# Sink probabilities, sink values and the order of a step in a sliding-window attention stage that runs ahead of two feed-forward layers

## The chip, the cores and the metric

The kernel runs on one core of a Trainium2 chip. The metric is the device time of one execution in microseconds, as the median of several runs.

## The reference, cut to what matters

```python
def _attn_ref(q, k, v, n_sink, window):          # q, k, v: (2, 8, 768, 64)
    scores = scale * np.matmul(q, k.transpose(0, 1, 3, 2))
    keep = (pos[None, :] < n_sink) | ((rel >= 0) & (rel < window))   # n_sink 4, window 128
    scores = np.where(keep, scores, -1000000000.0)
    a = np.exp(scores - np.max(scores, axis=-1, keepdims=True))
    a = a / (np.sum(a, axis=-1, keepdims=True) + 1e-09)
    return np.matmul(a, v)
x = attention rearranged to (1536, 512)
x = ((x @ w_a) * (x @ w_b)) @ w_out               # d_ff 1536
return np.maximum(x @ w_in, 0.0) ** 2 @ w_out2     # d_ff 2048
```

The feed-forward weights arrive as float64.

## The kernel before, in words

Attention is cut into 24 groups: a batch, a block of 128 queries, and four heads. A query block sees its own and the previous key block and the first eight keys, the sink. The loop of `attention_fast` runs steps g = 0 to 25. Each step works on several groups at once: `scores(g)` and `softmax(g, 0)`, `softmax(g, 1)`, the transposes of the probabilities of group g-1 (`probs`, `probs_copy`), the transposes of k and q of group g+1 (`transposes`), `normalize(g)`, the value products of group g-2 (`values`) and the transpose of the sink probabilities of g-1 (`probs_sink`). On TensorE, VectorE, ScalarE and GpSimd the order of the instructions in this stage is that of the program; the SP queue, which issues the loads, may be ordered otherwise.

In a softmax, VectorE selects the live triangle of the two key blocks in PSUM (L265), takes each head's maximum (L268), and ScalarE takes the exponential (L271). `normalize` (L280 to L288) divides on VectorE; GpSimd then splits the sink columns into two rounded parts (L287, L288). `probs_copy` copies the transposed probabilities on ScalarE (`th`, L302), and GpSimd cuts them into two triangles with two selects (`lu`, L309 and L311). The sink values are laid out once in `vs` (L183 to L207): two loads, splits on GpSimd, four matmuls that place them, two products on VectorE.

Two other works are woven into a step. First, the decode of the float64 weights, one tile of 128x512 in each step that `DECODE` lists: `W.stages` has ScalarE take a magnitude (L503), VectorE do four operations (L505 to L510), ScalarE cast the high part (`wh`, L515) and VectorE subtract it (`wl`, L517). The words `next(piece)` in the loop say where each part is issued. Second, `fill`, twice in a step: 12 matmuls of the first feed-forward layer (`psa`, L562) with one decoded tile. From step 6 on, when 256 tokens of attention are ready, each `fill` takes the next tile: tiles 0 and 1 in step 6, 2 and 3 in step 7, 4 and 5 in step 8, 6 and 7 in step 9. Its third matmul is the first to need `wl`. In every second `fill` VectorE multiplies the two results (`gs`, L576). Before step 6, and where no tokens are ready, `fill` issues two warming matmuls.

After the attention stage TensorE runs the feed-forward layers, and `W.ahead` decodes the remaining tiles, a third as often as TensorE's pieces come.

Of the kernel before, what the change touches and what calls it, by code (L numbers as in the profile page):

```python
# [18 lines left out]
P = 128  # L19
SK = 8  # L20
# [6 lines left out]
DECODE = (1, 2, 3, 4, 5, 6, 7, 8, 10, 12, 14, 16, 18, 20)  # L27
SINK = (0, 1, 3)
# [26 lines left out]
def setup(tc, cp, tp, n_sink, window):  # L55
    nc = tc.nc
    c = Attn()
    ident = tp.tile([P, P], F32, name="ident")
    make_identity(nc, ident)
    c.identr = cp.tile([P, P], F32R, name="identr")  # L60
    nc.vector.tensor_copy(c.identr, ident)
    c.ident = c.identr.bitcast(F32)

    raw = cp.tile([P, 4], I32, name="raw")
    nc.scalar.dma_start(raw[:, 0:2], n_sink.bitcast(I32).partition_broadcast(P))
    nc.scalar.dma_start(raw[:, 2:4], window.bitcast(I32).partition_broadcast(P))
    warm = tp.tile([P, 1], F32, name="warm")
    nc.scalar.activation(warm, c.ident[:, 0:1], AF.Exp)
    lo = cp.tile([P, 2], F32, name="lo_f")
    hi = cp.tile([P, 2], F32, name="hi_f")  # L70
    nc.vector.tensor_copy(lo, raw.bitcast(U32)[:, 0:4:2])
    nc.vector.tensor_copy(hi, raw[:, 1:4:2])
    par = cp.tile([P, 2], F32, name="par")
    nc.vector.scalar_tensor_tensor(out=par, in0=hi, scalar=4294967296.0, in1=lo, op0=ALU.mult, op1=ALU.add)
    c.ns = par[:, 0:1]
    c.w = par[:, 1:2]

    return c
# [51 lines left out]
def attention_fast(tc, ctx, c, rp, spare, q, k, v, xh, xl, fill, decode, warm):  # L130
# [54 lines left out]
    def sink_parts():
        for t, part, off in ((sel[0], slice(0, 64), slice(64, 96)), (sel[1], slice(64, 96), slice(0, 64))):
            t_ = t[:, part].rearrange("p (a s) -> p a s", s=SK)
            nc.gpsimd.tensor_copy(t_, c.ident[0:SK, 0:SK].unsqueeze(1).to_broadcast(t_.shape))
            nc.gpsimd.tensor_copy(t[:, off], c.ident[0:SK, P - (off.stop - off.start):P])
        nc.vector.tensor_reduce(out=own, in_=c.ident[0:96, 0:96].rearrange("p (k j s) -> p j k s", k=3, s=SK),  # L190
                                op=ALU.add, axis=AX.XY)

        vsr = raws.pop("s")
        for b in range(B):
            hi, lo = (t[0:SK] for t in spare[b])
            src = vsr[:, b].rearrange("p h d -> p (h d)")
            nc.gpsimd.tensor_copy(hi, src)
            nc.gpsimd.tensor_sub(lo, src, hi.bitcast(F32))

    def sink_values():  # L200
        for b in range(B):
            hi, lo = (t[0:SK] for t in spare[b])
            pt = ps_t.tile([P, 512], F32, name="pvs", tag="tr")
            nc.tensor.matmul(pt[0:96], lhsT=sel[0], rhs=hi, start=True, stop=False)
            nc.tensor.matmul(pt[0:96], lhsT=sel[1], rhs=lo, start=False, stop=True)
            nc.vector.tensor_mul(vs[:, b].rearrange("p (g q) (r d) -> p g (q r) d", g=2, r=2),
                                 pt[0:96].rearrange("p (g j d) -> p g j d", g=2, d=D),  # L207
                                 own.unsqueeze(1).unsqueeze(3).to_broadcast([96, 2, 4, D]))
# [231 lines left out]
class Weights:  # L440
# [7 lines left out]
    def __init__(self, tc, cp, rp, w_a, w_b, w_out, w_in2, w_out2):  # L448
# [30 lines left out]
        self.beat = 0  # L479

# [10 lines left out]
    def stages(self):  # L491

        while len(self.raws) < AHEAD and self.next < len(self.order):
# [9 lines left out]
        nc.scalar.activation(tf, up.bitcast(F32), AF.Abs)  # L503
# [3 lines left out]
                                op0=ALU.logical_shift_left, op1=ALU.bitwise_or)  # L507
        nc.vector.scalar_tensor_tensor(out=t, in0=up, scalar=0x3FFFFFFF, in1=t,  # L508
# [161 lines left out]
def sliding_window_moe_kernel(ctx, tc, q, k, v, n_sink, window, w_a, w_b, w_out, w_in2, w_out2, out):  # L670
# [16 lines left out]
    with tc.tile_pool(name="mk", bufs=1, side="right") as mk:  # L687
        c = setup(tc, cp, mk, n_sink, window)
        masks(tc, cp, mk, c)

    def run(attend):
# [3 lines left out]
        with ExitStack() as c0:  # L695
# [51 lines left out]
    run(lambda ctx, *work: attention_fast(tc, ctx, c, rp, first[-3:], q, k, v, xh, xl, *work))  # L747
# [39 lines left out]
```

## Time and profile before

| | |
|---|---|
| median of 3 runs (lowest, highest) | 687.59 us (687.39, 688.04) |
| the profiled execution, its own time | 688.03 us |
| its span, first to last instruction | 686.0 us |
| busy: TensorE, VectorE, ScalarE, GpSimd | 658.2, 406.0, 274.9, 48.8 us |

The profiled execution took 0.44 us more than the median, and 2.03 us of it lie outside the span. The busy times are sums over stages with different limits: the attention stage ends at 177 us, and from 200 us on TensorE is busy without a gap until the last stores.

### The profile page before, as it was taken

What the parts mean: (1) busy time and instruction counts of PE and PEld (TensorE: products, weight loads), DVE (VectorE), ACT (ScalarE), POOL (GpSimd) and SP (SyncE); (2) the same over time, 40 slices, a digit from 0 to 9 for tenths busy, and PEclk for the clock granted to TensorE, in tenths of its full rate; (3) what the DMA queues carried; (4) which work ended last, traced back from release to release, by engine and by line L of the source; (5) the groups of instructions that cost most, each with busy time, mean ns of one, the idle gap of its engine ahead of it and who ended that gap; (6) DMA issues with size and microseconds to landing.
All of it is one profiled execution on the core that took longest, in us unless ns stands there. A gap on an engine that the chain in (4) does not pass through costs nothing.

```text
span 686.0 us, 9622 instructions
## 1 busy us (share of the span) xinstructions
PE 658.2 (96%) x3582; PEld 546.0 (80%) x3582; DVE 406.0 (59%) x921; ACT 274.9 (40%) x638; POOL 48.8 (7%) x100
## 2 busy tenths in 40 slices
PE   6869999989999999999999999999999999999996
PEld 3557887878988888888888888888888888888884
DVE  5999778786688811389932599624933232323323
ACT  4565566564544511455521356234532222222221
POOL 3132222223000000000000000000000000000000
PEclk9799999999999999999999999999999999999999
DMA  9654343341065400044600024300200000001011
GB/s 193 167 134 125 101 116 87 108 116 32 16 194 159 152 5 0 1 135 145 189 23 1 28 86 136 119 1 27 67 1 0 1 0 1 1 0 62 11 51 66
DMA packets 65413, 48.96 MB, mean 71 GB/s; under 512 B 39760, under 2 KB 60240, under 8 KB 65360
## 3 DMA queue, kind: packets, MB, share of 16 engines
q1 hardware_dynamic: 65072, 48.28, 24.6%
q8 instruction: 30, 0.49, 0.3%
q14 instruction: 23, 0.19, 0.1%
q10 hardware_dynamic: 288, 0.00, 0.0%
HBM read 45.12 MB, written 3.15 MB: 70 GB/s over the span
## 4 chain that ended last, share of the span: by engine, by line
PE 88%; DVE 7%; DMA 2%; issue 1%; ACT 1%; SPq 0%; POOL 0%; DVEq 0%; POOLq 0%
PE psa L562 46%; PE acc L600 33%; PE x L330 2%; PE sc L250 2%; PE ptp L296 1%; DVE wtmp L508 1%; DVE ex L268 1%; DVE wtmp L510 1%; PE pt L226 1%; DVE sc L265 1%; PE x L335 1%; DVE ex L282 1%; DMA wraw<-in_moe_w_a_dram 1%; DVE wtmp L506 1%; DVE wtmp L505 1%
## 5 line engine op out<-in xcount | busy, mean ns | idle before, releaser
L562 PE MATMUL psa<-xh,wh 128*128 128x512 f32 (+1 forms) x576 | 206.3, 359 | 0.0
L562 PE MATMUL psa<-xl,wh 128*128 128x512 f32 (+1 forms) x576 | 203.4, 353 | 0.0
L562 PE MATMUL psa<-xh,wl 128*128 128x512 f32 (+1 forms) x576 | 203.2, 353 | 0.0
L562 PEld LDWEIGHTS psa<-xh,wh 128*128 128x128 f32 x576 | 108.6, 188 | 15.1 <-issue 0.2
L562 PEld LDWEIGHTS psa<-xl,wh 128*128 128x128 f32 x576 | 108.6, 189 | 14.9
L562 PEld LDWEIGHTS psa<-xh,wl 128*128 128x128 f32 x576 | 108.4, 188 | 14.9
L639 DVE TENSOR_TENSOR g<-u 128x512 f32<-128x512 f32 x48 | 33.2, 691 | 112.0 <-ACT u L629 112.0
L629 ACT ACTIVATE u<-psa 128x512 f32<-128x512 f32 x48 | 28.7, 598 | 120.0 <-PE psa L562 119.9
L51 ACT CAST gh<-g 128x512 fp32r<-128x512 f32 x72 | 44.7, 620 | 76.3 <-DVE g L636 42.1
L600 PE MATMUL acc<-wh,gl 128*128 128x512 f32 x192 | 74.7, 389 | 0.0
L600 PE MATMUL acc<-wl,gh 128*128 128x512 f32 x192 | 74.7, 389 | 0.0
L52 DVE TENSOR_TENSOR gl<-g,gh 128x512 fp32r<-128x512 f32 x72 | 49.7, 691 | 32.7 <-ACT gh L51 32.3
L503 ACT ACTIVATE wtmp<-wraw 128x512 f32<-128x512 f32 x68 | 45.5, 675 | 52.3 <-DMA wraw<-in_moe_w_in_dram 14.2
L600 PE MATMUL acc<-wh,gh 128*128 128x512 f32 x192 | 62.7, 389 | 0.0
L515 ACT CAST wh<-wtmp 128x512 fp32r<-128x512 f32 x68 | 41.7, 620 | 45.5 <-DVE wtmp L510 25.0
L600 PE MATMUL acc<-gl,wh 128*128 128x512 f32 x144 | 56.0, 389 | 0.0
L600 PE MATMUL acc<-gh,wl 128*128 128x512 f32 x144 | 56.0, 389 | 0.0
L517 DVE TENSOR_TENSOR wl<-wtmp,wh 128x512 fp32r<-128x512 f32 x68 | 46.5, 687 | 15.0 <-ACT wh L515 14.0
L271 ACT ACTIVATE ex<-ex,nb 128x136 f32<-128x136 f32 (+1 forms) x96 | 38.3, 400 | 42.3 <-DVE nb L268 42.3
L508 DVE SCALAR_TENSOR_TENSOR wtmp<-wraw,wtmp 128x512 int32<-128x512 int32 x68 | 50.2, 742 | 0.7
L600 PE MATMUL acc<-gh,wh 128*128 128x512 f32 x144 | 48.4, 389 | 0.0
L510 DVE SCALAR_TENSOR_TENSOR wtmp<-wraw,wtmp 128x512 int32<-128x512 int32 x68 | 47.5, 703 | 0.7
(96 smaller groups left out, 759.9 us busy)
## 6 DMA issues: line engine op xcount, KB each, us to landing
wraw<-in_moe_w_out_dram SPq DMA_DIRECT2D x28, 512.0 KB, 3.4
wraw<-in_moe_w_in_dram SPq DMA_DIRECT2D x16, 512.0 KB, 3.7
wraw<-in_moe_w_a_dram SPq DMA_DIRECT2D x12, 512.0 KB, 3.8
wraw<-in_moe_w_b_dram SPq DMA_DIRECT2D x12, 512.0 KB, 4.3
vraw<-in_v_dram SPq DMA_DIRECT2D x24, 128.0 KB, 3.3
out_dram<-part SPq DMA_DIRECT2D x12, 256.0 KB, 2.2
kraw<-in_k_dram SPq DMA_DIRECT2D x23, 128.0 KB, 2.4
qraw<-in_q_dram SPq DMA_DIRECT2D x23, 128.0 KB, 3.0
```

The costliest lines, as they stand in the source:

```text
L51: nc.scalar.copy(hi, src)
L52: (lo_eng or nc.vector).tensor_sub(lo, src, hi.bitcast(F32))
L271: nc.scalar.activation(ex[:, h, 0:w], ex[:, h, 0:w], AF.Exp, bias=nb[:, h:h + 1], scale=-1.0, accum_out=ss[:, h:h + 1])
L503: nc.scalar.activation(tf, up.bitcast(F32), AF.Abs)
L508: nc.vector.scalar_tensor_tensor(out=t, in0=up, scalar=0x3FFFFFFF, in1=t, op0=ALU.bitwise_or, op1=ALU.bitwise_and)
L510: nc.vector.scalar_tensor_tensor(out=t, in0=low, scalar=29, in1=t, op0=ALU.logical_shift_right, op1=ALU.bitwise_or)
L515: nc.scalar.copy(hi, tf)
L517: nc.vector.tensor_sub(lo, tf, hi.bitcast(F32))
L562: self.tc.nc.tensor.matmul(ps, lhsT=w[:, kt, :], rhs=x[:, kt, ts], start=n == 0, stop=n == 3 * KT - 1)
L600: mm = nc.tensor.matmul(acc[d], lhsT=a, rhs=b_, start=f == 0 and j == 0, stop=f == NF - 1 and j == 2)
L629: nc.scalar.activation(u, pa, AF.Relu)
L639: nc.vector.tensor_mul(g, u, u)
```

## The change

The sink probabilities are no longer split by GpSimd. VectorE writes three copies of them, already divided (`sp`, 128x96), TensorE transposes them in full float32, ScalarE rounds them to `st`, and VectorE subtracts in 32 rows what the rounding took (new L314). The sink values are placed by 24 small loads of 8 rows into a buffer that GpSimd sets to zero, with two casts and two subtractions in step 3 (`sink_split`). Of the division, VectorE does two heads and ScalarE two (new L276). The copy `th` stands ahead of the four exponentials. Of the decode, VectorE's two two-operand operations (L508, L510) move behind `normalize`. `DECODE` has 12 steps, from 2 to 9 and then 11, 13, 15, 17, where it had 14 from step 1. The loads of v are issued a step later, the two scalars are loaded to one partition and spread by a matmul, and the first three decodes after attention keep their place in the program on ScalarE (`PINNED`).

```diff
-DECODE = (1, 2, 3, 4, 5, 6, 7, 8, 10, 12, 14, 16, 18, 20)
-SINK = (0, 1, 3)
+DECODE = (2, 3, 4, 5, 6, 7, 8, 9, 11, 13, 15, 17)
+SINK = (1, 3)
+PINNED = 3
...
-    raw = cp.tile([P, 4], I32, name="raw")
-    nc.scalar.dma_start(raw[:, 0:2], n_sink.bitcast(I32).partition_broadcast(P))
-    nc.scalar.dma_start(raw[:, 2:4], window.bitcast(I32).partition_broadcast(P))
+    raw = cp.tile([1, 4], I32, name="raw")
+    nc.scalar.dma_start(raw[:, 0:2], n_sink.bitcast(I32).partition_broadcast(1))
+    nc.scalar.dma_start(raw[:, 2:4], window.bitcast(I32).partition_broadcast(1))
+    one = cp.tile([1, P], F32, name="one")
+    nc.vector.memset(one, 1.0)
+    par0 = cp.tile([1, 2], F32, name="par0")
+    nc.vector.scalar_tensor_tensor(out=par0, in0=hi, scalar=4294967296.0, in1=lo, op0=ALU.mult, op1=ALU.add)
+    ps = pp.tile([P, 2], F32, name="par_ps")
+    nc.tensor.matmul(ps, lhsT=one, rhs=par0, start=True, stop=True)
-    nc.vector.scalar_tensor_tensor(out=par, in0=hi, scalar=4294967296.0, in1=lo, op0=ALU.mult, op1=ALU.add)
+    nc.vector.tensor_copy(par, ps)
...
-        raws[g] = out
+        raws[g], raws[g, "v"] = out, out[2]
-            src = (q, k, v)[j][b, GH * m + h:GH * m + h + n, i * P:(i + 1) * P, :]
+            src = (q, k)[j][b, GH * m + h:GH * m + h + n, i * P:(i + 1) * P, :]
...
-        get(2, 0, GH)
+        for h in (g - 1, g) if g == N - 1 else (g - 1,):
+            if h >= 0:
+                bh, ih, mh = groups[h]
+                nc.sync.dma_start(raws[h, "v"], v[bh, GH * mh:GH * (mh + 1), ih * P:(ih + 1) * P, :]
+                                  .rearrange("h t d -> t h d"))
...
     vs = p1.tile([96, B, H // 2, P], F32R, name="vs")
-    sel = [t[0:SK, 0:12 * SK] for t in spare[B]]
-    own = p1.tile([96, 4], F32, name="own")
+    vsr = rp.tile([P, 512, 2], I32, name="wraw", tag="wraw", bufs=NRAW).rearrange("p n t -> p (n t)").bitcast(F32)
+    vsr = vsr[0:96, 0:B * (H // 2) * P].rearrange("p (b a c) -> p b a c", b=B, c=P)
     def sink_load():
-        vsr = rp.tile([P, 512, 2], I32, name="wraw", tag="wraw", bufs=NRAW).rearrange("p n t -> p (n t)")
-        raws["s"] = vsr = vsr.bitcast(F32)[0:SK].rearrange("p (b h d) -> p b h d", b=B, h=H)
+        nc.gpsimd.memset(vsr, 0.0)
+        for kind in range(3):
+            for j in range(GH):
+                for b in range(B):
+                    p0 = (kind * GH + j) * SK
+                    nc.sync.dma_start(vsr[p0:p0 + SK, b, j // 2:H // 2:2, (j % 2) * D:(j % 2 + 1) * D],
+                                      v[b, j:H:GH, 0:SK, :].rearrange("m s d -> s m d"))
+    def sink_split():
         for b in range(B):
-            nc.sync.dma_start(vsr[:, b], v[b, :, 0:SK, :].rearrange("h s d -> s h d"))
...
+            nc.scalar.copy(vs[:, b], vsr[:, b])
+            nc.vector.tensor_sub(vs[64:96, b], vsr[64:96, b], vs[64:96, b].bitcast(F32))
...
         if not 0 <= g < N:
             return
         ex, ss = pns[g][0:2]
-        i = groups[g][1]
-        w = P if i == 0 else SW
         nc.vector.tensor_scalar_add(ss, ss, 1e-9)
         nc.vector.reciprocal(ss, ss)
-        nc.vector.tensor_mul(ex[:, :, 0:w], ex[:, :, 0:w], ss.unsqueeze(2).to_broadcast([P, GH, w]))
-        if i > 0:
-            sps[g] = sp = p2.tile([P, 3, GH, SK], F32R, name="sp", tag="sp", bufs=NSP)
-            sn = ex[:, :, P:SW]
-            nc.gpsimd.tensor_copy(sp[:, 0:3:2], sn.unsqueeze(1).to_broadcast([P, 2, GH, SK]))
-            nc.gpsimd.tensor_sub(sp[:, 1], sn, sp[:, 0].bitcast(F32))
+        nc.vector.tensor_mul(ex[:, 0:2, 0:P], ex[:, 0:2, 0:P], ss[:, 0:2].unsqueeze(2).to_broadcast([P, 2, P]))
+        for h in range(2, GH):
+            nc.scalar.mul(ex[:, h, 0:P], ex[:, h, 0:P], ss[:, h:h + 1])
+        if groups[g][1] > 0:
+            sps[g] = p2.tile([P, 3, GH, SK], F32, name="sp", tag="sp", bufs=NSP)
+            nc.vector.tensor_mul(sps[g], ex[:, :, P:SW].unsqueeze(1).to_broadcast([P, 3, GH, SK]),
+                                 ss.unsqueeze(1).unsqueeze(3).to_broadcast([P, 3, GH, SK]))
     def probs(g):
         if not 0 <= g < N:
...
-        pt = ps_t.tile([P, GH, P], F32, name="pst", tag="tr")
-        nc.tensor.transpose(pt[0:96, 0, :].bitcast(F32R), sps.pop(g).rearrange("q k h s -> q (k h s)"), c.identr)
+        pt = ps_t.tile([P, GH, P], F32, name="pst", tag="tr")[0:96, 0, :]
+        nc.tensor.transpose(pt, sps.pop(g).rearrange("q k h s -> q (k h s)"), c.ident)
         st = sts[g] = p2.tile([96, P], F32R, name="st", tag="st", bufs=NSP)
-        nc.scalar.copy(st, pt[0:96, 0, :])
+        nc.scalar.copy(st, pt)
+        nc.vector.tensor_sub(st[32:64], pt[32:64], st[32:64].bitcast(F32))
 
     def values(g):
 
...
     for g in range(N + 2):
-        for sink, at in zip((sink_load, sink_parts, sink_values), SINK):
-            if g == at:
-                sink()
+        if g == SINK[0]:
+            sink_load()
         load(g + 2)
         piece = decode(g)
         next(piece)
         warm(WARM2.get(g, 0))
         scores(g)
-        softmax(g, 0)
         probs(g - 1)
         probs_copy(g - 1)
+        softmax(g, 0)
         softmax(g, 1)
+        if g == SINK[1]:
+            sink_split()
         fill(None)
         next(piece)
         transposes(g + 1)
         normalize(g)
+        next(piece)
         next(piece)
         values(g - 2)
         probs_sink(g - 1)
...
-        nc.scalar.activation(tf, up.bitcast(F32), AF.Abs)
+        a = nc.scalar.activation(tf, up.bitcast(F32), AF.Abs)
+        if pin:
+            self.tc.keep_in_program_order(a)
         yield
         nc.vector.tensor_scalar(out=tf, in0=tf, scalar1=WMIN, scalar2=WMAX, op0=ALU.max, op1=ALU.min)
         nc.vector.tensor_scalar(out=t, in0=t, scalar1=3, scalar2=-0x3FFFFFFF,
                                 op0=ALU.logical_shift_left, op1=ALU.bitwise_or)
+        yield
         nc.vector.scalar_tensor_tensor(out=t, in0=up, scalar=0x3FFFFFFF, in1=t,
                                        op0=ALU.bitwise_or, op1=ALU.bitwise_and)
         nc.vector.scalar_tensor_tensor(out=t, in0=low, scalar=29, in1=t,
...
-        for _ in self.stages():
+        for _ in self.stages(self.pinned > 0):
+        self.pinned -= 1
```

Three places show how the change moves instructions. The first is VectorE, from the end of the maxima to the end of the step that decodes tile 6 (step 7 before, step 8 in the change). Before:

```order
L505 TENSOR_SCALAR wtmp<-wtmp 128x512
L506 TENSOR_SCALAR wtmp<-wtmp 128x512
L508 SCALAR_TENSOR_TENSOR wtmp<-wraw,wtmp 128x512
L510 SCALAR_TENSOR_TENSOR wtmp<-wraw,wtmp 128x512
L280 TENSOR_SCALAR ss<-ss 128x4
L281 RECIPROCAL ss<-ss 128x4
L282 TENSOR_TENSOR ex<-ex,ss 128x544
L52 TENSOR_TENSOR xl<-x,xh 128x2x128
L517 TENSOR_TENSOR wl_82<-wtmp,wh_81 128x512
L576 TENSOR_TENSOR gs_153<-u,psa 128x256
```

In the change:

```order
L504 TENSOR_SCALAR wtmp<-wtmp 128x512
L505 TENSOR_SCALAR wtmp<-wtmp 128x512
L272 TENSOR_SCALAR ss<-ss 128x4
L273 RECIPROCAL ss<-ss 128x4
L274 TENSOR_TENSOR ex<-ex,ss 128x2x128
L280 TENSOR_TENSOR sp<-ex,ss 128x96
L508 SCALAR_TENSOR_TENSOR wtmp<-wraw,wtmp 128x512
L510 SCALAR_TENSOR_TENSOR wtmp<-wraw,wtmp 128x512
L53 TENSOR_TENSOR xl<-x,xh 128x2x128
L314 TENSOR_TENSOR st<-pst,st 32x128
L517 TENSOR_TENSOR wl_82<-wtmp,wh_81 128x512
L577 TENSOR_TENSOR gs_163<-u,psa 128x256
```

The division (`ss`, `ex`) and the new `sp` stand between the two halves of the decode, so that `xl` comes directly behind the decode's last two-operand operation; `st` is new ahead of `wl`.

The second is ScalarE in the same step. Before:

```order
L503 ACTIVATE wtmp<-wraw 128x512
L271 ACTIVATE ex,ss<-ex,nb 128x136 x2
L302 COPY th<-ptp 128x512
L271 ACTIVATE ex,ss<-ex,nb 128x136 x2
L573 COPY u<-psa 128x256
L228 COPY kq<-pt 128x2x2x128
L515 CAST wh_81<-wtmp 128x512
L51 CAST xh<-x 128x2x128
L320 CAST st<-pst 96x128
```

In the change:

```order
L500 ACTIVATE wtmp<-wraw 128x512
L295 COPY th<-ptp 128x512
L265 ACTIVATE ex,ss<-ex,nb 128x136 x4
L574 COPY u<-psa 128x256
L222 COPY kq<-pt 128x2x2x128
L276 ACTIVATE ex<-ex,ss 128x128 x2
L515 CAST wh_81<-wtmp 128x512
L52 CAST xh<-x 128x2x128
L313 CAST st<-pst 96x128
```

`th` now stands ahead of all four exponentials, two scalings of `ex` are new, and `xh` stands behind the cast `wh` in both.

The third is the SP queue, which issues the loads, from the sink values on before, and in the change from the load of k of group 4 on. Before:

```order
L183 DMA wraw<-in_v_dram 8x8x64 x2
L157 DMA kraw<-in_k_dram 128x4x64
L157 DMA qraw<-in_q_dram 128x4x64
L157 DMA vraw<-in_v_dram 128x4x64
L157 DMA kraw<-in_k_dram 128x4x64
L157 DMA qraw<-in_q_dram 128x4x64
L157 DMA vraw<-in_v_dram 128x4x64
L488 DMA wraw<-in_moe_w_a_dram 128x4x256
L488 DMA wraw<-in_moe_w_b_dram 128x4x256
```

In the change:

```order
L164 DMA kraw<-in_k_dram 128x4x64
L164 DMA qraw<-in_q_dram 128x4x64
L178 DMA vraw<-in_v_dram 128x4x64
L485 DMA wraw<-in_moe_w_a_dram 128x4x256
L485 DMA wraw<-in_moe_w_b_dram 128x4x256
L178 DMA vraw<-in_v_dram 128x4x64
L196 DMA wraw<-in_v_dram 8x2x64 x24
L164 DMA kraw<-in_k_dram 128x4x64
L164 DMA qraw<-in_q_dram 128x4x64
L485 DMA wraw<-in_moe_w_a_dram 128x4x256
```

The sink loads stood ahead of the first two weight tiles; now 24 stand behind these, and the loads of k and q of group 5 and the third weight tile behind the 24.

## Rows read from the trace of the kernel before

**Rows 1.** Windows view, attention from step 9 on: busy by engine, clock, DMA
```profile
69.00:176.00 107.00, 101.82 (x918) 88.04 (x918) 80.45 (x266) 61.30 (x212) 28.15 (x56) 1.00 0.34 88
```

**Rows 2.** Chain that ended last, TensorE pieces: start, us, what
```profile
73.23 1.49 PE psa L562 x12
...
79.75 1.50 PE psa L562 x12
...
176.88 23.20 PE psa L562 x147
```

**Rows 3.** Timeline of step 7: start, us, engine, line, operation
```profile
56.44 0.42 DVE L505 TENSOR_SCALAR wtmp<-wtmp 128x512 f32<-128x512 f32 x1
...
56.87 0.63 POOL L309 TENSOR_SCALAR_AFFINE_SELECT lu<-th 128x512 f32<-128x512 f32 x1 [2.48 <-ACT th L302]
56.90 0.89 DVE L506 TENSOR_SCALAR wtmp<-wtmp 128x512 int32<-128x512 int32 x1
...
57.46 0.82 POOL L311 TENSOR_SCALAR_AFFINE_SELECT lu<-th 128x512 f32<-128x512 f32 x1
...
57.82 1.00 DVE L508 SCALAR_TENSOR_TENSOR wtmp<-wraw,wtmp 128x512 int32<-128x512 int32 x1
...
58.86 0.69 DVE L510 SCALAR_TENSOR_TENSOR wtmp<-wraw,wtmp 128x512 int32<-128x512 int32 x1
...
59.47 0.16 DVE L280 TENSOR_SCALAR ss<-ss 128x4 f32<-128x4 f32 x1
...
59.58 0.62 ACT L515 CAST wh<-wtmp 128x512 fp32r<-128x512 f32 x1 [1.25 <-DVE wtmp L510]
...
59.88 0.72 DVE L282 TENSOR_TENSOR ex<-ex,ss 128x544 f32<-128x544 f32 x1
...
60.11 0.36 ACT L51 CAST xh<-x 128x256 fp32r<-128x256 f32 x1
...
60.52 0.42 DVE L52 TENSOR_TENSOR xl<-x,xh 128x256 fp32r<-128x256 f32 x1
...
60.85 0.69 DVE L517 TENSOR_TENSOR wl<-wtmp,wh 128x512 fp32r<-128x512 f32 x1
...
61.46 0.41 DVE L576 TENSOR_TENSOR gs<-u,psa 128x256 f32<-128x256 f32 x1
...
61.80 0.42 DVE L265 COPY_PREDICATED sc<-upi,sc 128x256 f32<-128x256 int32 x1
...
63.70 0.42 DVE L505 TENSOR_SCALAR wtmp<-wtmp 128x512 f32<-128x512 f32 x1
```

**Rows 4.** Timeline of step 2, two decode operations
```profile
21.67 0.43 DVE L506 TENSOR_SCALAR wtmp<-wtmp 128x512 int32<-128x512 int32 x1
...
22.13 0.69 DVE L508 SCALAR_TENSOR_TENSOR wtmp<-wraw,wtmp 128x512 int32<-128x512 int32 x1
```

**Rows 5.** Timeline of step 20, a select beside a maximum
```profile
144.80 0.78 POOL L309 TENSOR_SCALAR_AFFINE_SELECT lu<-th 128x512 f32<-128x512 f32 x1 [4.80 <-ACT th L302]
...
145.01 0.29 DVE L268 CUSTOM_DVE_ANT_0 ex<-sc,m 128x136 f32<-128x136 f32 x1
```

**Rows 6.** Timeline of ScalarE, first steps
```profile
6.45 0.58 ACT L228 COPY kq<-pt 128x512 f32<-128x512 f32 x1 [3.20 <-PE pt L226]
...
9.93 0.56 ACT L228 COPY kq<-pt 128x512 f32<-128x512 f32 x1
14.15 0.66 ACT L503 ACTIVATE wtmp<-wraw 128x512 f32<-128x512 f32 x1 [3.67 <-DMA wraw<-in_moe_w_a_dram]
```

**Rows 7.** The page, costliest groups: busy us, mean ns, idle before
```profile
L271 ACT ACTIVATE ex<-ex,nb 128x136 f32<-128x136 f32 (+1 forms) x96 | 38.3, 400 | 42.3 <-DVE nb L268 42.3
```

**Rows 8.** Timeline of the SP queue, sink loads
```profile
5.22 0.67 SPq L183 DMA_DIRECT2D wraw<-in_v_dram  x2
```

**Rows 9.** DMA view, first 40 us: count, KB each, us to landing
```profile
raw<-in_n_sink_dram ACTq DMA_DIRECT2D x1, 1.0 KB, 2.7
```

**Rows 10.** Timeline of ScalarE, start of step 20
```profile
139.09 1.81 ACT L503 ACTIVATE wtmp<-wraw 128x512 f32<-128x512 f32 x3
```

More of the change, by code (lines that the diff above doesn't have):

```diff
@@ L52, in split, with setup @@
     (lo_eng or nc.vector).tensor_sub(lo, src, hi.bitcast(F32))
-def setup(tc, cp, tp, n_sink, window):
+def setup(tc, cp, tp, pp, n_sink, window):
     nc = tc.nc
@@ L62, in setup @@
     c.ident = c.identr.bitcast(F32)
-    raw = cp.tile([P, 4], I32, name="raw")
-    nc.scalar.dma_start(raw[:, 0:2], n_sink.bitcast(I32).partition_broadcast(P))
-    nc.scalar.dma_start(raw[:, 2:4], window.bitcast(I32).partition_broadcast(P))
+    raw = cp.tile([1, 4], I32, name="raw")
+    nc.scalar.dma_start(raw[:, 0:2], n_sink.bitcast(I32).partition_broadcast(1))
+    nc.scalar.dma_start(raw[:, 2:4], window.bitcast(I32).partition_broadcast(1))
     warm = tp.tile([P, 1], F32, name="warm")
     nc.scalar.activation(warm, c.ident[:, 0:1], AF.Exp)
-    lo = cp.tile([P, 2], F32, name="lo_f")
-    hi = cp.tile([P, 2], F32, name="hi_f")
+    lo = cp.tile([1, 2], F32, name="lo_f")
+    hi = cp.tile([1, 2], F32, name="hi_f")
+    one = cp.tile([1, P], F32, name="one")
+    nc.vector.memset(one, 1.0)
     nc.vector.tensor_copy(lo, raw.bitcast(U32)[:, 0:4:2])
     nc.vector.tensor_copy(hi, raw[:, 1:4:2])
+    par0 = cp.tile([1, 2], F32, name="par0")
+    nc.vector.scalar_tensor_tensor(out=par0, in0=hi, scalar=4294967296.0, in1=lo, op0=ALU.mult, op1=ALU.add)
+    ps = pp.tile([P, 2], F32, name="par_ps")
+    nc.tensor.matmul(ps, lhsT=one, rhs=par0, start=True, stop=True)
     par = cp.tile([P, 2], F32, name="par")
-    nc.vector.scalar_tensor_tensor(out=par, in0=hi, scalar=4294967296.0, in1=lo, op0=ALU.mult, op1=ALU.add)
+    nc.vector.tensor_copy(par, ps)
     c.ns = par[:, 0:1]
@@ L127, in masks, with attention_fast @@
     nc.vector.tensor_copy(c.slow, f[:, 3:4])
-def attention_fast(tc, ctx, c, rp, spare, q, k, v, xh, xl, fill, decode, warm):
+def attention_fast(tc, ctx, c, rp, q, k, v, xh, xl, fill, decode, warm):
     nc = tc.nc
@@ L185, in sink_parts @@
[L185 to L208, printed above, removed]
+        nc.gpsimd.memset(vsr, 0.0)
@@ L479, in __init__ @@
         self.beat = 0
+        self.pinned = PINNED
     def load(self):
@@ L489, in load, with stages @@
             self.raws.append(raw)
-    def stages(self):
+    def stages(self, pin=False):
         while len(self.raws) < AHEAD and self.next < len(self.order):
@@ L686, in sliding_window_moe_kernel @@
     nc.vector.memset(zero, 0.0)
-    with tc.tile_pool(name="mk", bufs=1, side="right") as mk:
-        c = setup(tc, cp, mk, n_sink, window)
+    with tc.tile_pool(name="mk", bufs=1, side="right") as mk, \
+            tc.tile_pool(name="ps_m", bufs=1, space=PSUM, side="right") as ps_m:
+        c = setup(tc, cp, mk, ps_m, n_sink, window)
         masks(tc, cp, mk, c)
@@ L726, in decode @@
                     return W.stages()
-                return iter((None,) * 4)
+                return iter((None,) * 5)
             with ExitStack() as c1, tc.manual_schedule(engines=ORDERED):
@@ L745, in run @@
                                 W.ahead()
-    run(lambda ctx, *work: attention_fast(tc, ctx, c, rp, first[-3:], q, k, v, xh, xl, *work))
+    run(lambda ctx, *work: attention_fast(tc, ctx, c, rp, q, k, v, xh, xl, *work))
     slow = nc.values_load(c.slow[0:1, 0:1], min_val=0, max_val=1,
```

## The prediction

> **What bounds the kernel now.** I read the page first, then the windows of the attention stage, then the chain of waits, then the timeline of single steps. On the page TensorE is busy for 658 of 686 us, so what can be won is its idle time and the time in which it does warming work. From step 9 to the end of attention it is busy for 101.8 of 107 us [rows 1]: 5.2 us idle. The chain shows it as a stream of fills, the two of a step in a period of 6.52 us (73.23 to 79.75), with the second fill of step 9 at 73.23 and a stream without a gap from 176.88 on [rows 2]. Ahead of step 9 it is otherwise: the timeline shows VectorE without a gap through a whole decode step, which takes 7.26 us from one decode's first operation to the next (56.44 to 63.70) [rows 3]. So VectorE sets the pace until all eight tiles of the first layer are decoded, and TensorE sets it after that. One thing joins the two: a fill can't go past its third matmul before its tile's `wl` is there.
>
> **A decode step on VectorE.** In step 7 VectorE's starts are apart by: L505 0.46, L506 0.92, L508 1.04, L510 0.61, the sum and reciprocal 0.41, the division 0.64, `xl` 0.33, `wl` 0.61, `gs` 0.34, select and maxima 1.90; together 7.26 [rows 3].
>
> What the change removes. While GpSimd's selects run (56.87 to 58.28), L506 takes 0.89 and L508 1.00; without them 0.43 and 0.69 [rows 3, 4]. With `th` ahead of the exponentials the selects can start about 1.7 us earlier (two exponentials, a wait for the third), beside the maxima. One maximum that lies wholly beside a select took 0.29 us, no longer than the others [rows 5], so I let the selects cost nothing there, and the two operations fall back: L506 to 0.46 and L508 to 0.73 with their gaps, 0.77 us less.
>
> What it moves. Today sum, reciprocal and division (1.05 us) stand between L510 and `xl`, and cost nothing there: `xl` starts at 60.52, right when ScalarE's cast `xh` ends (60.11 + 0.36), and that stands behind the cast `wh`, which waits for L510 [rows 3]. From the start of L510 to `xl` it is 1.66 us with or without the division. In the change the division lies ahead of L508, so it is paid in full, and VectorE stands idle for 0.97 us behind L510 (59.55 to 60.52).
>
> What it adds. Half the division, 128x256: as `xl`, 0.33. `sp` (128x96) and the subtraction `st` (32x128) are not in this trace; by the nearest rows they lie between 0.20 (128x4, 59.47) and 0.33 (128x256), and with some hundred columns I take 0.25 each.
>
> The sum of a decode step in the change: maxima 1.90, L504 0.46, L505 0.46, sum and reciprocal 0.41, half division 0.33, `sp` 0.25, L508 0.73, L510 to `xl` 1.66, `xl` 0.33, `st` 0.25, `wl` 0.61, `gs` 0.34: **7.73 us, 0.47 more than today**. Steps 4 and 5 have no `gs`: 7.39. The uncertain prices move it by 0.1 down and 0.16 up.
>
> **When the eighth tile is ready.** Decode now starts in step 2. Step 1 without it no longer waits for its tile, as ScalarE does today until 14.15; its copy `kq` of step 0 was done from 9.93, 3.48 us after the one before [rows 6]. Step 1 adds `th` and two scalings to that, about 1 us, so `kq` of step 1 comes at 14.4, and the first select of step 2 at 15.2. Step 2 has no `st`, but its exponentials stand behind a magnitude and `th` and end some 0.6 us too late for VectorE: 7.7, to 22.9. In step 3 the two casts of the sink values follow the exponentials, four of 0.40 us [rows 7] that end some 0.8 us behind the maxima, and VectorE's two subtractions of 512 columns follow these, priced as `wl`: the step gets 2.75 us longer, 10.14, to 33.0. Steps 4 and 5 make 14.8 (47.8), steps 6 to 8 make 23.2 (71.0), and `wl` of step 9 ends 7.5 us into it, at **78.5**.
>
> Today the fill that needs it starts at 73.23, since its tile is decoded a step earlier. In the change tile 7 is decoded in step 9 itself, ahead of the second fill that wants it. TensorE does two matmuls (0.25 us) and waits: **5.0 us later than today**. Nothing gives that back, because TensorE's stream has no other gap to absorb it.
>
> **From there to the end of attention.** TensorE's 5.2 us of idle time, 4.8 of it behind 73.23, go: part of them are two decodes from behind the attention stage that are pulled into step 20 (three magnitudes in a row, at 139.09) [rows 10] and now stay in place, and part are steps after a decode. Four decode steps are left. VectorE needs about 8.2 us in each (7.73, and half a microsecond more as the exponentials now wait for `th`, a copy like `kq`, 0.56 [rows 6]) where TensorE needs 6.52. Of these 1.7 us the buffers take some; between 0 and 1.7 I take 0.95, 3.8 in all. The sink transpose in full float32 is not in this trace; I take 0.05 us more (nothing to 0.1, an estimate) in 14 steps: 0.7. Together **-0.3 us**, with bounds of -4.8 and +3.
>
> **What costs nothing.** GpSimd's zeroing lies beside step 1's maxima. v is loaded a step later but used three steps after its k. The matmul that spreads the two scalars stands ahead of the first transposes, which wait for k and q too; 0 to 0.5 us. The tiles that are decoded later (two that left `DECODE`, and those that were pulled forward) lie beside nine fills with ready tiles, 13 us [rows 2]; if that cover is too short, up to 3 us.
>
> **The sink loads.** Two sink loads were issued in 0.67 us [rows 8], so 24 take about 8; behind two weight tiles they start at about 14. A load of 1 KB landed after 2.7 us [rows 9], and as each waits for the one eight ahead of it in the queue, eight can be under way at a time, so the last lands at 24 to 26, when the casts of step 3 want them (25.6). I take no wait; bounds 0 and 3 us.
>
> The sum: 5.0 - 0.3 = 4.7 us on the profiled execution's 688.03, so 692.7. The median lies 0.44 below that execution: **692.3 us**.
>
> **The rivals.**
> *The wait behind the decode is not there* (0.23, faster). If VectorE did not stand idle between L510 and `xl`, each of eight steps were 0.97 shorter, `wl` of tile 7 ready at 70.7, ahead of its fill. The start of the fill would follow it, 2.8 us earlier than today, and the lag of four later decode steps would go: -2.8 - 4.1 = -6.9, 681 us; with half of it 686. It decides from about 0.4 us per step on. For it speaks that the changed order gives ScalarE its scalings early; against it that `xl` starts 0.05 us after `xh` today, behind the same cast.
> *No change* (0.14): the same with 0.3 to 0.5 us per step, about 688.
> *The sink data land late* (0.14). Each microsecond that step 3 waits for them moves everything behind by one: 3 us late, 695.3. For it: they stand right behind two weight tiles of 512 KB in one queue. Against it: they carry 4 KB each.
> *The selects don't move* (0.05). If `th` still comes late, the 0.77 us stay in seven steps: 697.7. Against it: the selects wait for `th` alone today (2.48 us in step 7) [rows 3].
> *The sink loads go one by one* (0.02). At 2.7 us each, 24 take 65 us, step 3 waits some 53 us, and the time is 745. Against it stands the pair that was issued within 0.67 us. The Trainium skill speaks for it, in DMA: Bandwidth & Descriptors, section Anatomy of one DMA — SWDGE (gpsimd) path: a transfer has a fixed part of about 2.0 us whatever its size, and the section Rules for kernel authors says to merge many small transfers, as those under 64 KB pay mostly overhead. By that figure, one after the other, an estimate of 48 us for the loads, and a step 3 that waits about 36; the pair of loads here bears out that the fixed part overlaps, and so I keep this at the chance above.
>
> **How the numbers follow.** A measurement tells about 0.2% from no change, 1.4 us, so 686.2 to 689.0 is the same. The forecast's mechanism at its price has 0.42, and with the three slower rivals slower has 0.63; the same 0.14; faster 0.23. The range leaves out the greater part of the first rival's gain and the last two rivals' upper ends: 684.5 to 697.
>
> **What would show it.** In the changed profile: L505 at 0.43 and L508 at 0.69 in steps 4 to 8, GpSimd's selects beside the maxima, VectorE idle for about a microsecond ahead of `xl` with ScalarE's `xh` as what ended it, first selects of a step 7.7 us apart, and TensorE waiting for `wl` in step 9 until about 78. If the second fill of step 9 starts before 74, the forecast is wrong, and the step length of the decode is where to look. No group of decode operations should stand inside step 20.

## The result and the profile after

The changed kernel took 693.1 us (median of 4 runs, 692.2 to 693.85); beside it the kernel before took 687.5. The ratio is 1.0079, with a 95% interval of 1.0062 to 1.0097: **slower by 0.8%**, about 5.5 us. Its profiled execution took 693.52 us.

The span of the changed kernel is 691.8 us; the busy time of each engine, from its page:

```profile
PE 660.8 (96%) x3580; PEld 547.9 (79%) x3580; DVE 401.7 (58%) x962; ACT 291.7 (42%) x688; POOL 28.0 (4%) x53
```

TensorE's busy time grew by 2.6 us (658.2 before) and the span by 5.8, so over half of the loss is waiting. Two steps of the timeline of the changed kernel, first step 3, which also splits the sink values, with the SP queue's row for their 24 loads ahead of it:

```profile
12.34 10.82 SPq L196 DMA_DIRECT2D wraw<-in_v_dram  x24
...
22.54 0.42 DVE L259 COPY_PREDICATED sc<-upi,sc 128x256 f32<-128x256 int32 x1
...
25.04 1.12 ACT L201 CAST vs<-wraw 96x512 fp32r<-96x512 f32 x2
...
25.67 1.28 DVE L202 TENSOR_TENSOR vs<-wraw,vs 32x512 fp32r<-32x512 f32 x2 [1.25 <-ACT vs L201]
...
32.57 0.43 DVE L259 COPY_PREDICATED sc<-upi,sc 128x256 f32<-128x256 int32 x1
```

The loads are all issued by 23.16, and the casts follow ScalarE's last exponential without a wait for one. VectorE is idle for 1.25 us until ScalarE's first cast of the sink values, then subtracts for 1.28. The step takes 10.03 us, from its first select (22.54) to the next step's (32.57). Then step 9, which decodes the eighth tile:

```profile
70.72 0.42 DVE L259 COPY_PREDICATED sc<-upi,sc 128x256 f32<-128x256 int32 x1
...
70.78 0.63 POOL L302 TENSOR_SCALAR_AFFINE_SELECT lu<-th 128x512 f32<-128x512 f32 x1 [6.54 <-ACT th L295]
...
71.41 0.29 DVE L262 CUSTOM_DVE_ANT_0 ex<-sc,m 128x136 f32<-128x136 f32 x1
...
72.98 0.43 DVE L505 TENSOR_SCALAR wtmp<-wtmp 128x512 int32<-128x512 int32 x1
...
74.28 0.68 DVE L508 SCALAR_TENSOR_TENSOR wtmp<-wraw,wtmp 128x512 int32<-128x512 int32 x1
75.00 0.69 DVE L510 SCALAR_TENSOR_TENSOR wtmp<-wraw,wtmp 128x512 int32<-128x512 int32 x1
75.72 0.62 ACT L515 CAST wh<-wtmp 128x512 fp32r<-128x512 f32 x1 [1.07 <-DVE wtmp L510]
...
76.25 0.36 ACT L52 CAST xh<-x 128x256 fp32r<-128x256 f32 x1
...
76.39 0.39 PE L563 MATMUL psa<-xh,wh 128*128 128x256 f32 x1 [1.97 <-ACT wh L515]
...
76.64 0.42 DVE L53 TENSOR_TENSOR xl<-x,xh 128x256 fp32r<-128x256 f32 x1 [0.96 <-ACT xh L52]
...
77.42 0.69 DVE L517 TENSOR_TENSOR wl<-wtmp,wh 128x512 fp32r<-128x512 f32 x1
...
78.16 0.58 PE L563 MATMUL psa<-xh,wl 128*128 128x256 f32 x1 [1.27 <-DVE wl L517]
```

Read it against [rows 3]; L504 and L505 are what was L505 and L506. GpSimd's selects now stand beside the maxima (70.78), a maximum beside one takes 0.29, and the decode's operations are at their undisturbed 0.43, 0.68 and 0.69. VectorE's starts from L510 to `xl` lie 1.64 us apart, 0.96 of it idle until `xh`, which stands behind `wh`. TensorE starts the second fill at 76.39, when `wh` is there, and its third matmul at 78.16, when `wl` is.

Three pieces of the chain of waits (start, us, what) say what this costs. The fills to compare are in [rows 2], and this one of the kernel before, the next behind the second fill of step 9:

```profile
76.43 1.43 PE psa L562 x12
```

In the changed kernel:

```profile
78.16 2.50 PE psa L563 x10
...
83.83 1.72 PE psa L563 x12
...
182.88 15.75 PE psa L563 x120
```

The third matmul of the second fill stands at 78.16, where the timeline of the kernel before has it at 73.38: 4.8 us later. The next fill, at 76.43 in the kernel before, stands at 83.83, 7.4 later; the stream without a gap starts at 182.88 instead of 176.88, 6.0 later. So 1.4 us come back on the way. The windows view, in the columns of [rows 1] (the clock third from the end), shows where more was lost than the wait itself:

```profile
74.00:76.00 2.00, 0.32 (x1) 0.12 (x1) 1.65 (x4) 0.93 (x4) 0.00 (x0) 1.00 0.54 123
76.00:78.00 2.00, 0.50 (x2) 0.30 (x2) 1.29 (x3) 0.77 (x3) 0.00 (x0) 0.89 0.60 193
78.00:80.00 2.00, 1.84 (x8) 1.84 (x9) 0.11 (x1) 0.00 (x0) 0.00 (x0) 0.50 0.17 70
...
82.00:84.00 2.00, 2.00 (x10) 1.30 (x9) 1.75 (x10) 0.08 (x1) 0.00 (x0) 0.50 0.00 0
```

From 74 to 78 TensorE works 0.82 of 4 us. Then the granted clock falls to 0.50, the lower of its two levels (1.2 instead of 2.4 GHz), for the 6 us that follow. The rest of the fill took 2.50 us for ten matmuls, where a whole fill of twelve takes 1.49 [rows 2], and the scores behind it 2.12 instead of 1.12.

### The profile page after: what moved, and what is told of

It is laid out like the page before. It is cut to its first block, busy times and chain, and to the rows that moved or that the text cites. A ratio compares the mean times of both kernels' runs of the same rounds, so it can differ in the third digit from the quotient of the medians.

```text
span 691.8 us, 9595 instructions
## 1 busy us (share of the span) xinstructions
PE 660.8 (96%) x3580; PEld 547.9 (79%) x3580; DVE 401.7 (58%) x962; ACT 291.7 (42%) x688; POOL 28.0 (4%) x53
## 4 chain that ended last, share of the span: by engine, by line
PE 83%; DVE 11%; ACT 4%; issue 1%; ACTq 0%; DVEq 0%
PE psa L563 44%; PE acc L601 33%; PE sc L244 2%; ACT ex L265 2%; DVE ex L262 2%; DVE wtmp L510 1%; PE x L324 1%; DVE sc L259 1%; DVE wl L517 1%; ACT wh L515 1%; DVE wtmp L508 1%; PE ptp L289 1%; PE psw L711 1%; DVE xl L53 1%; DVE wtmp L505 1%
## 5 line engine op out<-in xcount | busy, mean ns | idle before, releaser
L517 DVE TENSOR_TENSOR wl<-wtmp,wh 128x512 fp32r<-128x512 f32 x68 | 46.5, 687 | 15.2 <-ACT wh L515 13.9
L510 DVE SCALAR_TENSOR_TENSOR wtmp<-wraw,wtmp 128x512 int32<-128x512 int32 x68 | 46.6, 686 | 0.6
L508 DVE SCALAR_TENSOR_TENSOR wtmp<-wraw,wtmp 128x512 int32<-128x512 int32 x68 | 46.4, 685 | 0.2
L601 PEld LDWEIGHTS acc<-wh,gl 128*128 128x128 f32 x192 | 36.1, 188 | 7.5
```

The costliest lines, as they stand in the source:

```text
L510: nc.vector.scalar_tensor_tensor(out=t, in0=low, scalar=29, in1=t, op0=ALU.logical_shift_right, op1=ALU.bitwise_or)
L517: nc.vector.tensor_sub(lo, tf, hi.bitcast(F32))
L601: mm = nc.tensor.matmul(acc[d], lhsT=a, rhs=b_, start=f == 0 and j == 0, stop=f == NF - 1 and j == 2)
```

## The experiments

Ratios are to the kernel before, run on the same chip, with 95% intervals. Theory A is the prediction's own: longer decode steps, 0.97 us of each an idle wait, make the eighth tile late.

**The decode's four operations together again.**

```diff
                                 op0=ALU.logical_shift_left, op1=ALU.bitwise_or)
-        yield
...
         next(piece)
-        next(piece)
         values(g - 2)
```

> One part undone: the decode's four VectorE operations stand together again ahead of the division. Theory A (the late eighth tile comes from longer decode steps, 0.97 us of each being VectorE's wait for xh behind the cast wh): the division covers that wait again, a decode step falls from 7.75 to about 6.8 us, the third matmul of the second fill of step 9 starts near 72 to 73 instead of 78.16, the clock stays up behind it, and the time is about 684 us (681 to 687). Theory B (the added work costs: 24 loads, sink split, scalings on ScalarE, transposes in full float32; the order is harmless): the step gets at most 0.3 shorter and the time stays at 690 or more.

693.96 us, ratio 1.0087 (1.0070 to 1.0104): no gain at all. Theory A as I had put it fell. Step 7 in the timeline of this kernel:

```profile
58.70 0.69 DVE L508 SCALAR_TENSOR_TENSOR wtmp<-wraw,wtmp 128x512 int32<-128x512 int32 x1
...
59.77 0.70 ACT L276 ACTIVATE ex<-ex,ss 128x128 f32<-128x128 f32 x2 [1.19 <-DVE ss L273]
...
60.37 0.60 ACT L513 CAST wh<-wtmp 128x512 fp32r<-128x512 f32 x1
60.88 0.36 ACT L52 CAST xh<-x 128x256 fp32r<-128x256 f32 x1
...
61.27 0.42 DVE L53 TENSOR_TENSOR xl<-x,xh 128x256 fp32r<-128x256 f32 x1 [0.97 <-ACT xh L52]
```

The idle time is still there, 0.97 us ahead of `xl`, and from the decode's last operation to `xl` it is now 2.57 us, although the division stands behind L508 (here the decode's last operation) as it did before. What is new on ScalarE stands between: the two scalings (59.77) wait for the reciprocal, and `wh` (60.37) and `xh` follow them. In the kernel before `wh` ran beside the division [rows 3]; here it can't.

**Theory C: ScalarE's order decides.** Whatever stands ahead of `xh` on ScalarE is VectorE's wait. Two runs test it from two sides. First, the split decode stays, and `xh` and `st` go ahead of `wh`:

```diff
         next(piece)
-        next(piece)
         values(g - 2)
         probs_sink(g - 1)
         next(piece)
+        next(piece)
```

> The split of the decode stays, but the casts xh and st are issued on ScalarE ahead of the cast wh, so that VectorE can do xl and st while wh is cast. VectorE's own order is the same as in the changed kernel. Theory A: the idle 0.97 us ahead of xl goes, a decode step is 6.75 us, and the time is as with the decode whole, 682 to 687 us. Rival (the wait only moves: wl waits for wh instead): the step stays above 7.4 and the time at 691 to 693.

681.83 us, ratio 0.9917 (0.9901 to 0.9934): 11 us less than the change, and faster than the kernel before. VectorE's order is the same as in the changed kernel. Step 9 in its timeline, then its chain:

```profile
68.09 0.36 ACT L52 CAST xh<-x 128x256 fp32r<-128x256 f32 x1
...
68.65 0.69 DVE L510 SCALAR_TENSOR_TENSOR wtmp<-wraw,wtmp 128x512 int32<-128x512 int32 x1
69.26 0.41 DVE L53 TENSOR_TENSOR xl<-x,xh 128x256 fp32r<-128x256 f32 x1
69.37 0.62 ACT L515 CAST wh<-wtmp 128x512 fp32r<-128x512 f32 x1 [0.77 <-DVE wtmp L510]
...
70.02 0.69 DVE L517 TENSOR_TENSOR wl<-wtmp,wh 128x512 fp32r<-128x512 f32 x1
```

```profile
70.77 2.50 PE psa L563 x10
...
170.83 15.75 PE psa L563 x120
```

`xh` and `st` run beside L508, `xl` follows L510 at once, and `xl` and the subtraction of `st` cover the cast `wh`. Steps 4 to 8 take 6.4 to 6.8 us, the eighth tile's third matmul stands at 70.77, and the last stream starts 12 us earlier than in the changed kernel: 7.4 are won up to that matmul, and 3.4 of the rest behind the next fill (75.21 in its chain), where the later decode steps lie. Whether `xh` alone, without `st`, would do as well was not tried.

Second, the whole decode, its diff as above, with the division of all heads back on VectorE:

```diff
-        nc.vector.tensor_mul(ex[:, 0:2, 0:P], ex[:, 0:2, 0:P], ss[:, 0:2].unsqueeze(2).to_broadcast([P, 2, P]))
-        for h in range(2, GH):
-            nc.scalar.mul(ex[:, h, 0:P], ex[:, h, 0:P], ss[:, h:h + 1])
+        nc.vector.tensor_mul(ex[:, :, 0:P], ex[:, :, 0:P], ss.unsqueeze(2).to_broadcast([P, GH, P]))
```

> The decode's four VectorE operations together ahead of the division, as in the kernel with the whole decode, and now the division of all four heads on VectorE as well, so that ScalarE has no scalings ahead of wh. Theory C (in the kernel with the whole decode the two scalings, which wait for the reciprocal, stood ahead of wh on ScalarE and so the division no longer covered the cast): wh starts within 0.1 us of the end of L510, VectorE's idle time ahead of xl is under 0.1 us, a decode step is about 7.0 us, and the time is 682 to 687. Rival B (the added work costs, whatever the order): VectorE has 0.3 us more per step, so 693 or more.

685.05 us, ratio 0.9957 (0.9940 to 0.9973), 9 us below the run with the whole decode alone. VectorE does more here, and the kernel is faster. Step 9:

```profile
69.12 0.69 DVE L506 SCALAR_TENSOR_TENSOR wtmp<-wraw,wtmp 128x512 int32<-128x512 int32 x1
...
69.85 0.62 ACT L511 CAST wh<-wtmp 128x512 fp32r<-128x512 f32 x1 [0.84 <-DVE wtmp L506]
...
70.14 0.69 DVE L274 TENSOR_TENSOR ex<-ex,ss 128x512 f32<-128x512 f32 x1
...
70.92 0.42 DVE L53 TENSOR_TENSOR xl<-x,xh 128x256 fp32r<-128x256 f32 x1
```

`wh` starts with the end of L506 (the decode's last operation), beside the division, and nothing waits ahead of `xl`. So the half of the division that went to ScalarE is what took the cover away in that order.

**The same order in the kernel before**, where the division covers the cast:

```diff
         normalize(g)
-        next(piece)
         values(g - 2)
+        next(piece)
         probs_sink(g - 1)
```

> The kernel before with xh issued ahead of the cast wh, nothing else. If it is the division behind L510 that covers the cast there: no gain, 687 to 688.5, the step stays at 7.26. Rival (the wait behind the cast costs the kernel before as well): 684 or less.

687.99 us, ratio 0.9997 (0.9988 to 1.0007): nothing to gain there. The wait is a product of the change.

**Is the start of the decode in step 2 a cause of its own?** The sink values get a buffer of their own here, as otherwise they would hold one of the three that the weights use:

```diff
-DECODE = (2, 3, 4, 5, 6, 7, 8, 9, 11, 13, 15, 17)
+DECODE = (1, 2, 3, 4, 5, 6, 7, 8, 11, 13, 15, 17)
...
+    sk = ctx.enter_context(tc.tile_pool(name="sk", bufs=1))
...
-    vsr = rp.tile([P, 512, 2], I32, name="wraw", tag="wraw", bufs=NRAW)
+    vsr = sk.tile([P, 512, 2], I32, name="vsr")
```

> DECODE starts in step 1 again (1 to 8, then 11, 13, 15, 17), with a buffer of its own for the sink values. Theory A with the late start as a cause: step 2 begins at about 19.8 instead of 15.1, since step 1 waits for its weight tile, but the eighth tile is decoded in step 8, its wl ends near 75 instead of 78.1, and the time is 688 to 690. Rival (only the length of the steps counts, and the start gives back what it takes): tile ready at 77 or later, time 692 to 693.

690.77 us, ratio 1.0042 (1.0028 to 1.0056), just outside what I expected. Timeline, step 9:

```profile
73.11 0.69 DVE L518 TENSOR_TENSOR wl<-wtmp,wh 128x512 fp32r<-128x512 f32 x1
...
77.56 0.32 PE L312 MATMUL pst<-identr,sp 128*96 128x128 f32 x1 [0.83 <-ACT kq L223]
...
77.96 0.29 PE L564 MATMUL psa<-xh,wl 128*128 128x256 f32 x1
```

The eighth `wl` ends before 74, a step ahead of its use, and still the third matmul of the fill stands at 77.96, only 0.2 earlier. It is the step that is late: step 1 now waits for its weight tile (ScalarE's magnitude starts at 12.89, after 1.96 us of waiting for the load), step 2 starts at 19.06 instead of 15.07, and step 9 at 74.18 instead of 70.72. What this run gains is mostly the clock, which stays at 1.00, as TensorE is idle for 0.83 us there: the next fill stands at 81.02, 2.8 earlier than in the changed kernel.

**The clock.**

```diff
         next(piece)
+        if g == 9:
+            warm(26)
         fill(groups[g - 2][:2] if ...
```

> 26 warming matmuls ahead of the second fill of step 9, where TensorE waits for the eighth tile; nothing else is changed. Theory A with the clock (part of the cost is the granted clock of 0.50 in 78 to 84, behind a stretch in which TensorE was nearly idle): the third matmul still starts at about 78.2, the clock stays near 1 from 78 on, the fill takes 1.3 instead of 2.5 us, and the time falls by 2 to 3 us, to 690 to 691. Rival (VectorE sets the pace there anyway, so the slow clock costs nothing): no change, 693.

691.56 us, ratio 1.0047 (1.0031 to 1.0064), just above the range I expected. Windows of this kernel, and the last piece of its chain to compare:

```profile
76.00:78.00 2.00, 2.00 (x14) 1.17 (x13) 1.18 (x3) 0.89 (x3) 0.00 (x0) 1.00 0.45 150
78.00:80.00 2.00, 1.96 (x16) 1.57 (x15) 0.22 (x1) 0.00 (x0) 0.00 (x0) 1.00 0.32 121
...
180.84 15.75 PE psa L565 x120
```

The fill starts only at 78.72, behind the 26 matmuls, which were a few too many (`wl` is there at 78.2), and runs at full clock; 12 matmuls take 1.67. The stream from which there is no gap starts at 180.84, 2.0 us earlier than in the changed kernel. The time falls by 1.5 us in the medians and 2.2 by the ratios, whose intervals just touch. So the slow clock was a cost of its own; the trace shows it more clearly than the time.

**The copy `th` back between the halves.**

```diff
+        softmax(g, 0)
         probs(g - 1)
         probs_copy(g - 1)
-        softmax(g, 0)
         softmax(g, 1)
```

> The copy th is put back between the two softmax halves, the rest is as changed. If the selects beside the decode's first operations cost what the timeline of before shows (L506 0.89 and L508 1.00 instead of 0.43 and 0.69): L505 and a neighbour take 0.3 to 0.8 us more, the step is 8.2 to 8.5 us and the time 696 to 698. Rival (the collision falls into time in which VectorE would wait for ScalarE anyway): 692 to 694.

699.57 us, ratio 1.0163 (1.0146 to 1.0180), more than I expected. Step 8:

```profile
68.69 0.63 POOL L302 TENSOR_SCALAR_AFFINE_SELECT lu<-th 128x512 f32<-128x512 f32 x1 [7.21 <-ACT th L295]
68.72 0.88 DVE L505 TENSOR_SCALAR wtmp<-wtmp 128x512 int32<-128x512 int32 x1
...
69.52 0.59 DVE L272 TENSOR_SCALAR ss<-ss 128x4 f32<-128x4 f32 x1
```

L505 takes 0.88 beside the selects, and the sum (L272) 0.59 where it takes 0.17 alone; step 8 is 8.62 us instead of 7.75, and these two make up the 0.87.

**And that part alone in the kernel before:**

```diff
-        softmax(g, 0)
         probs(g - 1)
         probs_copy(g - 1)
+        softmax(g, 0)
         softmax(g, 1)
```

> The kernel before with one part of the change alone: the copy th ahead of both softmax halves, so that the selects run beside the maxima. If the collision of the selects with the decode is worth 0.77 us a step and nothing takes its place: a decode step falls from 7.26 to about 6.5 us, the second fill of step 9 starts 4 to 5 us earlier than 73.23, and the time is 682.5 to 685. Rival (the exponentials, now behind th, end later and VectorE waits for their sums): the step stays above 7 and the time at 686.5 to 688.

684.22 us, ratio 0.9946 (0.9929 to 0.9963). The copy ahead of the exponentials is worth 4 us by itself. Steps 4 and 5 fall to 6.3 and 6.2 us. Steps 6 to 8 fall only to between 6.9 and 7.15, above the 6.5 I expected, and the second fill of step 9 starts at 70.64, 2.6 us earlier and not 4 to 5. Step 7 shows why:

```profile
53.90 0.59 ACT L302 COPY th<-ptp 128x512 f32<-128x512 f32 x1 [1.80 <-PE ptp L296]
...
54.71 0.77 DVE L505 TENSOR_SCALAR wtmp<-wtmp 128x512 f32<-128x512 f32 x1
```

Here `th` waits for the transposes on TensorE (`ptp`), so the selects start at 54.56, and L505 beside them takes 0.77. In steps 6 to 8 of this kernel the collision is moved, not gone; in the changed kernel it is gone there.

**The pinned decodes.**

```diff
-PINNED = 3
+PINNED = 0
```

> The changed kernel with PINNED at 0: the first decodes behind attention may be pulled forward on ScalarE again. If their staying in place is worth what the prediction's sum counts on: a group of magnitudes stands inside one of the last steps, TensorE has 2 to 3 us more idle time between 140 and 185, and the time is 695 to 696. Rival (TensorE has buffers enough to hide them): 693 to 694.

701.66 us, ratio 1.0195 (1.0178 to 1.0212): 8.6 us more than the changed kernel, about three times what I expected. Three lines of the timeline late in attention:

```profile
127.47 1.79 ACT L500 ACTIVATE wtmp<-wraw 128x512 f32<-128x512 f32 x3
...
139.68 0.66 ACT L500 ACTIVATE wtmp<-wraw 128x512 f32<-128x512 f32 x1 [1.89 <-DMA wraw<-in_moe_w_a_dram]
...
142.13 1.12 PE L289 MATMUL ptp<-identr,ex 128*128 128x128 f32 x4 [4.01 <-DVE xl L53]
```

Three magnitudes come together in the middle of attention, VectorE's part of them lies among the maxima, a later one waits for its load, `xl` comes late, and TensorE waits 4.01 us for it. This step takes 14.40 us instead of 8.46. Here a second reason for a wait is pulled in by the scheduler; in the changed kernel the pins are worth these 8.6 us. What the pulled decodes cost in the kernel before, where they stand in step 20, was not tried.

**The sink split on GpSimd**, which is idle there:

```diff
-            nc.scalar.copy(vs[:, b], vsr[:, b])
-            nc.vector.tensor_sub(vs[64:96, b], vsr[64:96, b], vs[64:96, b].bitcast(F32))
+            nc.gpsimd.tensor_copy(vs[:, b], vsr[:, b])
+            nc.gpsimd.tensor_sub(vs[64:96, b], vsr[64:96, b], vs[64:96, b].bitcast(F32))
```

> The sink values are rounded and subtracted on GpSimd instead of ScalarE and VectorE; the 24 loads stay. If the 24 loads are on time and only the split costs: step 3 falls from 10.0 to about 7.5 us, everything behind it is 2.5 us earlier, and the time is 690 to 691. Rival (the 24 loads are late, or GpSimd beside VectorE slows it as much): step 3 stays above 9 and the time at 692 to 693.5.

692.76 us, ratio 1.0066 (1.0049 to 1.0082): no gain that can be told. Step 3:

```profile
23.61 0.61 POOL L201 CAST vs<-wraw 96x512 fp32r<-96x512 f32 x1 [0.36 <-POOL lu L304]
...
24.31 1.32 POOL L202 TENSOR_TENSOR vs<-wraw,vs 32x512 fp32r<-32x512 f32 x1
...
24.54 1.37 DVE L505 TENSOR_SCALAR wtmp<-wtmp 128x512 int32<-128x512 int32 x1
...
26.65 1.35 DVE L274 TENSOR_TENSOR ex<-ex,ss 128x256 f32<-128x256 f32 x1
```

The first cast starts 0.36 us behind a select; the row doesn't tell whether it waited for a load, but loads can have cost no more than that here. Beside GpSimd's work L505 takes 1.37 instead of 0.43, the sum 0.57 instead of 0.17, the half division 1.35 instead of 0.42: the step stays at 10.05. L505 ends at 25.91, 0.28 us behind the subtraction that it stood beside, and the half division at 28.00, again 0.28 behind GpSimd's second one (26.46 to 27.72). The Trainium skill has a rule for it, in SBUF — State Buffer, section Summary: rules for kernel authors: if VectorE works in a mode that takes both its ports, or reads two inputs from SBUF while GpSimd reads there too, the second of the two to issue is held until the first has finished. The half division reads two such inputs, and these ends agree with the rule; in which mode L505 ran, no row shows.

**What beats both.** `xh` and `st` ahead of `wh`, the split on GpSimd, and 13 warming matmuls in step 9; the diffs of the first two as above, and:

```diff
         next(piece)
+        if g == 9:
+            warm(13)
         fill(groups[g - 2][:2] if ...
```

> Three of the edits together: xh and st ahead of wh, the sink split on GpSimd, and 13 warming matmuls ahead of the second fill of step 9. If the three savings add up (11.3 from the first, 2.5 from the second, 1.3 to 1.5 from the clock in step 9): 677 to 679. Rival (TensorE is the bound from step 6 on and only the first 60 us can still be shortened, so that they overlap): 680 to 682.

680.54 us, ratio 0.9887 (0.9870 to 0.9903). That is the rival's time: the savings don't add up. The split gives nothing, as the run above shows (step 3 is 9.06 us here, 8.99 with `xh` and `st` first alone), and the warming 1 to 2 us.

The same with the split on ScalarE and VectorE again, but behind `wl` at the end of step 3:

```diff
         softmax(g, 1)
-        if g == SINK[1]:
-            sink_split()
         fill(None)
...
         next(piece)
+        if g == SINK[1]:
+            sink_split()
         if g == 9:
```

> xh and st ahead of wh, 13 warming matmuls ahead of the second fill of step 9, and the sink split back on ScalarE and VectorE but behind wl at the end of step 3, instead of ahead of the decode. If VectorE's wait of 1.25 us for the first sink cast is all that this place costs: step 3 falls from 9.0 to about 7.7 us and the time is 678.5 to 680. Rival (ScalarE's magnitude and th of step 4 wait behind the casts and give it back): 680.5 or more.

679.59 us, ratio 0.9880 (0.9863 to 0.9896); the interval overlaps that of the three together. Step 3 is what was expected, 7.69 us from its first select (22.38) to the next (30.07).

## Why the prediction was right, and where it was not

*Contention of the selects.* Right: L505 and L508 at 0.43 and 0.68, the maxima not slowed. Two runs price the place of `th` at 4 us in the kernel before, where it ends the collision in part, and about 6 in the changed one.

*The length of a decode step.* Forecast 7.73 and 7.39 without `gs`; measured 7.75 and 7.43. The idle time is 0.96, the half division 0.34 from start to start, `sp` 0.17 and `st` 0.32, priced at 0.33, 0.25 and 0.25.

*The reason for that length.* Half wrong. The wait is the one that was forecast: VectorE idle for 0.96 us until `xh`, which stands behind `wh`, which waits for L510. But the prediction put the loss on the place of the division, and said that from L510 to `xl` it is 1.66 us "with or without the division". The run with the whole decode shows 2.57 there: moving the division back brings nothing while ScalarE scales two heads ahead of `wh`. The cause is ScalarE's order. That the removal of the wait gives about 681, as the first rival said, is shown by 681.83. Its sum was 6.9 us below the kernel before; the last stream starts 6.0 earlier (170.83 against 176.88).

*When the eighth tile is ready.* Right in size: first selects at 15.07, 22.54, 32.57, 47.44, 70.72 (forecast 15.2, 22.9, 33.0, 47.8, 71.0), third matmul at 78.16 (78.5). In this kernel the fill does wait for its tile (1.27 us at 78.16). But the tile's own date is not the whole reason: with the decode a step earlier the fill came as late, because step 9 itself did.

*From there to the end.* Forecast -0.3; measured from 83.83 to 182.88 it is -1.4, within the bounds; TensorE's idle time on the way is 3.5 us, where it was 4.7. That the pinned decodes stay in place was counted as a part of a few microseconds; the run without it says 8.6 in the changed kernel. The sink transposes in full float32 take 0.31 us on average where they took 0.23, so 0.08 each instead of the 0.05 taken, for which the kernel before has no row.

*The missing term.* The clock. TensorE's wait in step 9 was priced as its length alone, 5.0 us. It measured 4.8, and the slow fill and scores behind it made 7.4 of it. With the -1.4 the sum is 6.0 where the forecast had 4.7; the two misses partly cancel in the time (693.1 against 692.3), so the closeness of the time is in part luck.

*Sink loads, wait at the start.* Right: no wait for the loads, step 3 at 10.03 (10.14). The 24 took 10.82 us to issue instead of about 8, and started at 12.34 instead of 14.

*Rivals.* Late sink data, unmoved selects and loads one by one (65 us) are excluded by the rows of steps 3 and 9.

## What to carry to other kernels

When part of an engine's work is moved to another, look at what stands behind it there: 0.7 us of scalings on ScalarE, ahead of a cast that others wait for, cost more than VectorE saved (693.96 against 685.05, both with the whole decode). On engines that work in program order, put the short operation that someone waits for (`xh`, `st`) ahead of the long one that itself waits (`wh`). A second engine is no cover if the two slow each other: the sink split on GpSimd beside VectorE gave back all that it took over.

## What I had not expected of the hardware

The wait of TensorE in step 9 cost more than its length: after 4 us with 0.82 us of work the granted clock stood at 0.50 for the next 6 us, and keeping the engine busy with matmuls whose result nobody reads took 2.0 us off the end of attention. And GpSimd's cast and subtraction made VectorE's operations about three times as long (1.37 and 1.35 us), a 128x4 sum included (0.57 instead of 0.17).
